# List scatters of the router placed behind three named stages of the scan loop, with a 388-word clearing between them

## The chip, the cores and the metric

The kernel runs on one core of a Trainium2 chip. The metric is the device time of one execution in microseconds (us); lower is better. The core has five engines that run at the same time, each working through its own instructions in order: PE (matrix multiply; its weight loads are shown apart as PEld), DVE (vector operations), ACT (activations and copies), POOL (a general engine, which here also issues all indirect DMAs) and SP (issues the plain DMAs). Sixteen DMA engines carry out the transfers.

## The reference

Two blocks follow each other. The first is a gated linear recurrence over 4 batches of 8 heads, 768 steps, head size 48. The second is a router that sends each of the 3072 resulting rows to two of eight experts.

```python
for t in range(S):                       # attention block
    state = f[:, :, t, :, None] * state + einsum('bhd,bhde' of k_t, v_t)
    y[:, :, t] = einsum('bhd,bhde->bhe', q[:, :, t], state)
x = y.transpose(0, 2, 1, 3).reshape(3072, 384)
noisy = x @ w_gate + log1p(exp(x @ w_noise)) * noise
top2  = the two largest of each row; top2_w = their softmax
for e in range(8):
    out[rows of e] += top2_w * (relu(x[rows] @ w1[e]) @ w2[e])
```

with `f = sigmoid(f_logit)`, w1 of 384 x 1024 and w2 of 1024 x 384 for each expert.

## The kernel before

**The scan loop.** The sequence is cut into 6 chunks of 128 steps; with 4 batches this makes 24 blocks, numbered n = 4 * chunk + batch. The main loop (L1496 to L1566) runs over i and calls, in each turn, seven stages, each for a block of its own (n = i minus the stage's lag): `forget` (transposes of the gate logits on PE, L534, and their logarithm on ACT), `scaled`, `scores`, `summed` (a running sum on DVE, the scan of L548, whose two inputs both lie in SBUF), `output` (PE products of values, L592, and of the carried state, L603, and then the new state on POOL, L619 and L620), `decays`, and `features` (PE product L627, rows to HBM). Behind `forget` stands `clamp` (L528 on POOL), which bounds the gate logits of a later block. The carried state is one per batch: block 23 reads what block 19 wrote, called `st_19` below.

**The lists.** After the four blocks of a chunk, `route(c)`, a generator of which each stage slot runs a step, picks the two experts of every row and their places in the experts' lists. Each chunk then has eight list scatters: `put` (L709) is an indirect DMA on POOL (L711) that writes 128 entries of 16 bytes, and behind each stands a small clearing on POOL: of one word for chunks 0 to 2 (`spacer`, L723), of 388 words in each partition for chunks 3 to 5 (`empty`, L725). The content of both is used by nothing afterwards.

**What sets the order.** Instructions stand on every engine in the order in which the Python code issues them. The loop has a running number `slot` of stage slots, and the condition of L1545 says after which of them a waiting scatter is issued: before the change, every third slot, and every second one once `n_routed` is 3 (= `HALF`) or a first fetch of a list has been issued. When the 24 scatters of chunks 0 to 2 are out, the generator `first_loads` (L1459) issues, some slots later: the fetch of the first list (L872, SP), the eight scatters of chunk 3 in one run, the two gathers of the first list's rows (`xg0`, L885, POOL), and 18 slots on their transposes on PE (`xgp0_0`, `xgp0_1`, L922; the copy behind them, L923, on DVE). Then come the first pieces of the expert part (`hp0_0`, L977).

**The expert part** takes about three quarters of the time; it goes through 256-row pieces of the lists, with the sums of Strassen-like products on DVE and ACT, and scatters the weighted result into `out`.

Of the kernel before, what the change touches and what calls it, by code (L numbers as in the profile page):

```python
# [332 lines left out]
def kernel(  # L333
# [51 lines left out]
    HALF = NCH // 2  # L385
# [133 lines left out]
    def load(nm, n):  # L519
        c, b = n // B, n % B  # L520
        if n < NCH * B:
            nc.sync.dma_start(out=pads[nm][n % RING[nm]][:, :, 0:D],
                              in_={"f": f_logit, "q": q, "k": k, "v": v}[nm][b, :, c * C:(c + 1) * C, :].rearrange("h t d -> t h d"))

    def clamp(n, engine=nc.gpsimd):
        if n < NCH * B:
            raw = pads["f"][n % RING["f"]][:, :, 0:D]
            engine.tensor_scalar(raw, raw, XMIN, None, ALU.max)  # L528
# [107 lines left out]
    def route(c):  # L636
        def t(shape, tag, dtype=F32):
            return rt.tile([128] + shape, dtype, tag=tag, name=f"{tag}_{c}")
# [65 lines left out]
        slot = t([2, B], "slot")  # L704
# [4 lines left out]
        def put(b, r):  # L709
            n_put.append(c)  # L710
            into = nc.gpsimd.indirect_dma_start(  # L711
                out=lists, out_offset=bass.IndirectOffsetOnAxis(ap=sloti[:, r, b:b + 1], axis=0),
                in_=entry[:, c, b, r, :], in_offset=None)
            tc.declare_no_dep(into.ins, group="lists", reason="slots differ")
            tc.add_to_no_dep_group("lists", into.ins)
            if c >= HALF:
                tc.declare_no_dep(into.ins, group="full", reason="slots differ")
                tc.add_to_no_dep_group("later", into.ins)
            if c == NCH - 1:
                tc.declare_no_dep(into.ins, group="nearly full", reason="slots differ")  # L720

            if c < HALF:
                nc.gpsimd.memset(spacer, 0.0)  # L723
            else:
                nc.gpsimd.memset(empty[:, 0:LR // 256], 0)  # L725
# [222 lines left out]
    done = {"fetch": 0, "gather": 0, 1: NR, 2: NR, "turned": False, "joint": False}  # L948
# [502 lines left out]
    def may_put():  # L1451
        return puts and (len(n_put) < HALF * B * 2 or done["fetch"] > (len(n_put) >= (NCH - 2) * B * 2))

    def second_slots():
        fetch(1)
        done["fetch"] = 2
        gather(1, (0,))
# [36 lines left out]
    slot = n_routed = n_first = 0  # L1494
    pieces = chain.from_iterable(((k, i) for i, _ in enumerate(first_layer(k) if k < NE else first_of_three(k))) for k in range(len(items)))
    for i in range(-3, NS + 2):  # L1496
# [5 lines left out]
        for stage, lag in order:  # L1502
            n = i - lag
            if not 0 <= n < NS:
                continue
            stage(n)
            if stage is forget:
                for m in () if n < 2 else (n + 3,) if n < 5 else (n + 3, n + 4) if n == 5 else (n + 4,):
                    load("f", m)
                if n > 1:  # L1510
                    clamp(n + 2)
                if n == 5:
                    tables()
            elif stage is scaled:
                for nm in "qk":
                    load(nm, n + 2) if n < 4 else load(nm, n + 3)
                    if n == 3:
                        load(nm, n + 3)
                if n < 2:
                    load("v", n)  # L1520
            elif stage is scores:
                for m in () if n == 0 else (n + 1,) if n < 4 else (2 * n - 3, 2 * n - 2) if n < 6 else (n + 3,):
                    load("v", m)
                if n in (2, 6, 7, 8, 9, 10):
                    load_router(2 + (2, 6, 7, 8, 9, 10).index(n))
                elif n == 5:
                    nc.sync.dma_start(out=lists.rearrange("(p r) w -> p r w", p=128), in_=empty)
            elif stage is summed and n == 0:
                clamp(2, nc.vector)
            elif stage is output:  # L1530
                while xw:
                    xw.pop(0)()
                if 9 <= n < 17:
                    part_of_weights(0, 1 + (n - 9) // 4, (n - 9) % 4)
                if n == NS - 3:
                    second_slots()
            elif stage is features and NS - 4 <= n < NS - 1:
                if n < NS - 2:
                    for part in range(2):
                        part_of_weights(1, 1, (n - NS + 4) * 2 + part)  # L1540
                zeros(4)
            for _ in range(2 if n_routed >= NCH - 1 else 1):
                next(router, None)
            slot += 1
            if may_put() and slot % (2 if n_routed == HALF or done["fetch"] else 3) == 0:  # L1545
                put_next()
            next(first_pairs, None)

            if done["turned"] and (n_first < 5 or i >= NS - 3 and stage is not forget) and (n_first < 11 or i >= NS - 1):
                next(pieces)  # L1550
                n_first += 1
# [6 lines left out]
        if n >= 0 and n % B == B - 1:  # L1558
            c = n // B
            router = chain(router, route(c))  # L1560
            n_routed = c + 1
# [104 lines left out]
```

## Time and profile before

| | us |
|---|---|
| three timed executions | 616.18, 619.41, 618.79 |
| their median | 618.79 |
| the profiled execution, its own time | 617.76 |
| its span, first to last instruction | 615.7 |
| busy in the span: PE, PEld | 602.0, 553.0 |
| busy in the span: DVE, ACT, POOL | 451.9, 377.8, 290.9 |
| the 48 list scatters on POOL (L711) | 52.8 |
| the 24 one-word and 24 388-word clearings behind them | 2.1 and 10.6 |

The profile is of one execution. Its span is 2.1 us shorter than that execution's time; what lies around the span is taken as fixed. Its rows give the start and the duration of instructions, and behind them in brackets how long the engine was idle before and what ended the idle time ("issue" means that nothing shown in the profile held it). TensorE's granted clock is 0.996 over the span.

### The profile page before, as it was taken

The page shows a single profiled execution, that of the slowest core. Times are in us where ns is not written, and L with a number is a line of the kernel's source. Part 1 is how long each engine was busy: PE and PEld are TensorE (multiplying, and loading weights), DVE is VectorE, ACT ScalarE, POOL GpSimd, SP SyncE. Part 2 cuts the span into 40 slices and gives each one's busy share as a digit, 9 for nine tenths or more (in the row PEclk, how much of TensorE's full clock was granted, in tenths as well). Part 3 has the DMA queues.
Part 4 walks back from the last instruction along what each step waited for, and adds up shares of the span by engine and source line. Part 5 has one row for each costly group of instructions (what it writes and reads, how often), then busy time and mean ns, then how long its engine had stood idle before and what let it go on. Part 6 is the DMA issues. An engine that isn't in the chain of part 4 may idle for free.

```text
span 615.7 us, 13343 instructions
## 1 busy us (share of the span) xinstructions
PE 602.0 (98%) x4830; PEld 553.0 (90%) x4830; DVE 451.9 (73%) x1056; ACT 377.8 (61%) x920; POOL 290.9 (47%) x316
## 2 busy tenths in 40 slices
PE   8999999999999999999999999999999999999995
PEld 7999998887999988998898899889988998998994
DVE  7777878778665488878777778787777777877840
ACT  6877676754222587667666755775577567647611
POOL 7724688878887550451062335414540624242032
PEclk9999999999999999999999999999999999999998
DMA  9999887996973874686489279839874893361024
GB/s 185 187 200 213 174 173 158 206 190 162 327 193 87 142 195 138 142 165 212 138 196 263 65 197 170 259 136 185 159 215 128 199 250 84 82 136 20 2 27 56
DMA packets 186219, 98.79 MB, mean 160 GB/s; under 512 B 150736, under 2 KB 179408, under 8 KB 186144
## 3 DMA queue, kind: packets, MB, share of 16 engines
q1 hardware_dynamic: 173968, 78.59, 51.2%
q0 software_dynamic: 12176, 19.25, 17.2%
q8 instruction: 40, 0.66, 0.4%
q14 instruction: 35, 0.29, 0.2%
HBM read 69.68 MB, written 19.62 MB: 145 GB/s over the span
## 4 chain that ended last, share of the span: by engine, by line
PE 82%; DMA 6%; issue 3%; POOL 3%; ACT 2%; DVE 2%; POOLq 0%; ACTq 0%
PE y L1218 27%; PE E L1052 8%; PE D L1052 8%; PE B L1052 6%; PE C L1052 6%; PE hp L977 5%; PE y L1162 3%; DMA x_rows<-xs 3%; PE sc L574 3%; PE y L592 3%; PE xp L627 2%; PE A L1052 2%; DMA xg<-hs_b 2%; PE fp L534 1%; POOL lists L711 1%
## 5 line engine op out<-in xcount | busy, mean ns | idle before, releaser
L1099 POOL DMA_INDIRECT out_dram<-ys,slots x48 | 91.1, 1898 | 216.0 <-DVE ys L1224 167.6
L1218 PE MATMUL y<-qk_all,f_all 128*128 128x192 f32 x504 | 88.8, 326 | 0.0
L1218 PEld LDWEIGHTS y<-qk_all,f_all 128*128 128x128 f32 x504 | 83.1, 190 | 0.0
L885 POOL DMA_INDIRECT xg<-x_rows,slots x48 | 52.5, 1093 | 36.0 <-DMA slots<-lists 18.8
L1060 ACT ACTIVATE hs_b<-hs_b 128x256 f32<-128x256 f32 x140 | 58.5, 418 | 6.9 <-DVE hs_b L1064 5.2
L1224 DVE SCALAR_TENSOR_TENSOR ys<-y,slots,ys 128x192 f32<-128x192 f32 x63 | 26.1, 415 | 49.1 <-PE y L1218 16.4
L1218 PE MATMUL y<-w,hs_b 128*128 128x192 f32 x336 | 61.5, 326 | 0.0
L711 POOL DMA_INDIRECT lists<-entry,sloti x48 | 52.8, 1101 | 8.7 <-issue 7.4
L1218 PEld LDWEIGHTS y<-w,hs_b 128*128 128x128 f32 x336 | 56.0, 190 | 0.4
L1267 ACT ACTIVATE ys<-y,slots 128x192 f32<-128x192 f32 x21 | 8.9, 421 | 59.5 <-PE y L1218 55.7
L577 DVE TENSOR_TENSOR A<-sc,causal 128x1024 f32<-128x1024 f32 x24 | 29.3, 1221 | 9.0 <-PE sc L574 8.5
L607 ACT COPY yT<-y 128x256 f32<-128x256 f32 x48 | 15.7, 376 | 29.8 <-PE y L603 21.4
L1057 ACT COPY hs_a<-D 128x256 f32<-128x256 f32 x77 | 28.5, 371 | 8.4 <-PE D L1052 4.5
L1218 PE MATMUL y<-qk_all,hs_b 128*128 128x192 f32 x168 | 31.5, 331 | 0.3 <-ACT ys L1239 0.2
L936 ACT COPY planes<-xg 128x768 uint16<-128x768 uint16 x36 | 29.6, 825 | 3.4 <-DMA xg<-x_rows,slots 2.8
L1218 PE MATMUL y<-w,f_all 128*128 128x192 f32 x168 | 31.3, 329 | 0.0
L548 DVE TENSOR_TENSOR_SCAN L<-f,cap 128x512 f32<-128x512 f32 x24 | 29.3, 1221 | 1.4 <-ACT cap L543 1.4
L1057 ACT COPY hs_a<-E 128x256 f32<-128x256 f32 x63 | 23.5, 372 | 10.8 <-PE E L1052 9.5
L1218 PEld LDWEIGHTS y<-qk_all,hs_b 128*128 128x128 f32 x168 | 27.4, 190 | 3.0 <-issue 2.1
L528 POOL TENSOR_SCALAR f_all<-f_all 128x384 f32<-128x384 f32 x21 | 26.4, 1257 | 5.0 <-DMA f_all<-in_f_logit_dram 2.7
L1087 DVE TENSOR_TENSOR f_all<-hs_b 128x512 f32<-128x512 f32 x42 | 28.7, 682 | 0.0
L1218 PEld LDWEIGHTS y<-w,f_all 128*128 128x128 f32 x168 | 27.6, 190 | 0.7
(273 smaller groups left out, 1593.4 us busy)
## 6 DMA issues: line engine op xcount, KB each, us to landing
w<-in_moe_w_dram SPq DMA_DIRECT2D x12, 1536.0 KB
w_q<-in_moe_w_dram SPq DMA_DIRECT2D x10, 1536.0 KB
w<-in_moe_w_dram SPq DMA_DIRECT2D x16, 384.0 KB
f_all<-in_f_logit_dram SPq DMA_DIRECT2D x24, 192.0 KB
qk_all<-in_q_dram SPq DMA_DIRECT2D x24, 192.0 KB
qk_all<-in_k_dram SPq DMA_DIRECT2D x24, 192.0 KB
v_all<-in_v_dram SPq DMA_DIRECT2D x24, 192.0 KB
x_rows<-xs SPq DMA_DIRECT2D x24, 192.0 KB
```

Source lines behind the costliest of these rows:

```text
L548: nc.vector.tensor_tensor_scan(L[n], data0=logf[n], data1=cap[n % 2].rearrange("d a t -> d (a t)"), initial=0.0, op0=ALU.add, op1=ALU.min)
L577: nc.vector.tensor_tensor(A[n].rearrange("j r (a i) -> j (r a) i", i=C), sc.rearrange("j r (a i) -> j (r a) i", i=C), causal.unsqueeze(1). ...
L711: into = nc.gpsimd.indirect_dma_start(out=lists, out_offset=bass.IndirectOffsetOnAxis(ap=sloti[:, r, b:b + 1], axis=0), in_=entry[:, c, b, ...
L885: nc.gpsimd.indirect_dma_start(out=xg[p][:, s, :], out_offset=None, in_=x_rows[0:(known(p) + (p == 1 and s)) * B * C], in_offset=bass.Indi ...
L936: nc.scalar.copy(planes[p][:, s], by_halves(p)[:, s * 2 * DM:(s + 1) * 2 * DM].rearrange("t (d h) -> t h d", h=2))
L977: nc.tensor.matmul(hp[:, o, :], lhsT=w1[home(k)][:, i, (fo + o) * 128:(fo + o + 1) * 128], rhs=rows_of(k)[:, i, :], start=(i == 0), stop=( ...
L1052: nc.tensor.matmul(banks[name, j], lhsT=half_of(x, k)[:, j * 128:(j + 1) * 128], rhs=half_of(y, k), start=first, stop=True, skip_group_che ...
L1057: nc.scalar.copy(at(to, j), banks[more[0], j])
L1060: nc.scalar.activation(at(to, j), at(y, j), AF.Relu, scale=-1.0 if more[0][0] == "-" else 1.0)
L1087: nc.vector.tensor_tensor(sm[which], x, y, op)
L1099: into = nc.gpsimd.indirect_dma_start(out=out, out_offset=bass.IndirectOffsetOnAxis(ap=slots[p][:, s, 2:3], axis=0), in_=ys[s], in_offset= ...
L1218: nc.tensor.matmul(to, lhsT=x[:, o, :], rhs=y[:, o, :], start=(start and o == 0), stop=(o == FH - 1), skip_group_check=not start)
```

## The change

Two lines are changed.

```diff
--- before.py
+++ after.py
@@ -719,7 +719,7 @@
             if c == NCH - 1:
                 tc.declare_no_dep(into.ins, group="nearly full", reason="slots differ")
 
-            if c < HALF:
+            if c == 0:
                 nc.gpsimd.memset(spacer, 0.0)
             else:
                 nc.gpsimd.memset(empty[:, 0:LR // 256], 0)
@@ -1542,7 +1542,7 @@
             for _ in range(2 if n_routed >= NCH - 1 else 1):
                 next(router, None)
             slot += 1
-            if may_put() and slot % (2 if n_routed == HALF or done["fetch"] else 3) == 0:
+            if may_put() and (slot % 2 == 0 if done["fetch"] else stage in (forget, output) or n_routed >= HALF and stage is summed):
                 put_next()
             next(first_pairs, None)
 
```

The first takes the 388-word clearing for chunks 1 and 2 too. The second ties the scatters of chunks 0 to 2 to stages: one behind `forget` and its clamp and one behind `output` in each turn of the loop, and a third behind `summed` once three chunks are routed. The seven stages of a turn gave 2.33 scatters before (3.5 with the shorter step); now they give 2, and later 3. No instruction is added or taken away but for the 16 clearings that are larger; 714 rows stand on POOL before and after.

On POOL, in the turns of chunk 1, the order was this (`sloti_1` holds the places of chunk 1's entries; f_all is a clamp; mid and st are the state of a block):

```order
L528 TENSOR_SCALAR f_all_95<-f_all_95 128x8x48
L711 DMA lists_136<-entry_142,sloti_1_1563 24832x4
L723 MEMSET spacer_147 1x1
L619 TENSOR_TENSOR mid_12_1659<-dss_12_1656,st_8_1195 128x256
L620 TENSOR_TENSOR st_12_1658<-mid_12_1659,P_12_1321 128x256
L711 DMA lists_136<-entry_142,sloti_1_1563 24832x4
L723 MEMSET spacer_147 1x1
L528 TENSOR_SCALAR f_all_95<-f_all_95 128x8x48
L711 DMA lists_136<-entry_142,sloti_1_1563 24832x4
L723 MEMSET spacer_147 1x1
```

Two scatters of chunk 1 stood ahead of the second clamp shown here. In the changed kernel the rows from that same clamp on are these:

```order
L528 TENSOR_SCALAR f_all_95<-f_all_95 128x8x48
L711 DMA lists_136<-entry_142,sloti_1_1561 24832x4
L725 MEMSET empty_137 128x388
L711 DMA lists_136<-entry_142,sloti_1_1561 24832x4
L725 MEMSET empty_137 128x388
L619 TENSOR_TENSOR mid_13_1771<-dss_13_1768,st_9_1311 128x256
L620 TENSOR_TENSOR st_13_1770<-mid_13_1771,P_13_1443 128x256
L711 DMA lists_136<-entry_142,sloti_1_1561 24832x4
L725 MEMSET empty_137 128x388
```

So chunk 1's scatters begin one turn of the loop later (chunk 0's eight now fill the turn before), and all sixteen of chunks 1 and 2 stand between this clamp and the first scatter of chunk 3, where fourteen stood before. From the first scatter of chunk 3 on, POOL's order is the same in both kernels; in both, block 19's state stands behind chunk 3's eight scatters and the two gathers. The end of that run reads, in both:

```order
L711 DMA lists_136<-entry_142,sloti_3_2396 24832x4
L725 MEMSET empty_137 128x388
L885 DMA xg0_2441<-x_rows_135,slots0_2370 128x384
L888 MEMSET empty_137 128x388
L885 DMA xg0_2441<-x_rows_135,slots0_2370 128x384
L888 MEMSET empty_137 128x388
L619 TENSOR_TENSOR mid_19_2481<-dss_19_2478,st_15_2007 128x256
L620 TENSOR_TENSOR st_19_2480<-mid_19_2481,P_19_2127 128x256
L885 DMA xg1_2622<-x_rows_135,slots1_2620 128x384
```

The last scatter of chunk 2 is issued in a later slot than before, and with it `first_loads` and all that it paces. On PE, at the end of the scan loop, the order before was:

```order
L627 MATMUL xp_21_2699<-w_rt_143,yT_21_2616 128x112 x4
L922 MATMUL xgp0_0_2713<-ident_90,xg0_2429 128x128 x3
L592 MATMUL y0_23_2719<-A_23_2660,v_all_97 64x128 x2
...
L603 MATMUL y0_23_2719<-qP_23_2560,st_19_2480 64x128 x2
...
L697 MATMUL rk_4_2740<-each_4_2667,earlier_131 128x32
...
L922 MATMUL xgp0_1_2752<-ident_90,xg0_2429 128x128 x3
L627 MATMUL xp_22_2757<-w_rt_143,yT_22_2695 128x112 x4
L977 MATMUL hp0_0_2770<-xt_a_152,w1_0_148 128x256 x6
```

and it is now:

```order
L627 MATMUL xp_21_2699<-w_rt_143,yT_21_2616 128x112 x4
L592 MATMUL y0_23_2714<-A_23_2660,v_all_97 64x128 x2
...
L603 MATMUL y0_23_2714<-qP_23_2560,st_19_2480 64x128 x2
...
L697 MATMUL rk_4_2735<-each_4_2667,earlier_131 128x32
...
L922 MATMUL xgp0_0_2747<-ident_90,xg0_2441 128x128 x3
L627 MATMUL xp_22_2752<-w_rt_143,yT_22_2695 128x112 x4
L922 MATMUL xgp0_1_2765<-ident_90,xg0_2441 128x128 x3
L627 MATMUL xp_23_2771<-w_rt_143,yT_23_2732 128x112 x4
...
L977 MATMUL hp0_0_2788<-xt_a_152,w1_0_148 128x256 x6
```

The transposes of the gathered rows moved behind block 23's output, which reads `st_19`, and the first expert product `hp0_0` moved behind the last `xp`. The order on SP did not change.

## The prediction

> **What bounds the kernel now.** I read the page's busy times first, then the waits of PE, then the timelines of POOL, DVE and PE around the places where the order changes.
>
> ```profile
> span 615.7 us, 13343 instructions
> PE 602.0 (98%) x4830; PEld 553.0 (90%) x4830; DVE 451.9 (73%) x1056; ACT 377.8 (61%) x920; POOL 290.9 (47%) x316
> PE xgp L922 <- DMA xg<-x_rows,slots: 0.8, 1, 0.8
> PE hp L977 <- DVE xt_a L923: 0.3, 1, 0.3
> ```
>
> PE is busy for 98% of the span, and no PE instruction is added or removed. The time can therefore change only by what PE waits. The two waits shown are the ones in the region that the change reaches: PE waits 0.80 us for the first gathered rows and 0.27 us for their copy. That is 1.07 us in all, and no more can be gained there. What can be lost has no such bound, since PE's work behind this place follows in one chain to the end.
>
> Where these waits lie, on PE, and the POOL run that feeds them:
>
> ```profile
> 147.06 1.15 PE L627 MATMUL xp<-w_rt,yT 128*128 128x112 f32 x8
> 149.01 0.52 PE L922 MATMUL xgp<-ident,xg 128*128 128x128 f32 x3 [0.80 <-DMA xg<-x_rows,slots]
> 149.46 1.09 PE L592 MATMUL y<-A,v_all 128*64 128x128 f32 x16
> 150.48 0.67 PE L603 MATMUL y<-qP,st 64*64 64x128 f32 x16
> 130.03 1.00 POOL L619 TENSOR_TENSOR mid<-dss,st 128x256 f32<-128x256 f32 x1 [1.63 <-ACT dss L612]
> 132.03 1.01 POOL L711 DMA_INDIRECT lists<-entry,sloti  x1 [0.30 <-DVE sloti L707]
> 133.04 0.45 POOL L725 MEMSET empty<- 128x388 uint32 x1
> 133.66 0.98 POOL L711 DMA_INDIRECT lists<-entry,sloti  x1 [0.17 <-issue]
> 145.14 0.99 POOL L885 DMA_INDIRECT xg<-x_rows,slots  x1 [0.16 <-issue]
> 148.89 0.62 POOL L620 TENSOR_TENSOR st<-mid,P 128x256 f32<-128x256 f32 x1
> ```
>
> POOL runs without a pause from 132.03: eight scatters of chunk 3, two gathers, and then block 19's state, `st_19`, done at 148.89 + 0.62 = 149.51. PE's L603 of block 23 reads that state at 150.48, only 0.97 us later. The view shows no wait there, because the wait for the gather stands in front of it.
>
> **The change, part by part.** *The larger clearing and the later start.* For POOL I take the stretch from the clamp at 92.65 (the one with which the second and third order rows begin) to chunk 3's first scatter at 132.03:
>
> ```profile
> 92.65 1.19 POOL L528 TENSOR_SCALAR f_all<-f_all 128x384 f32<-128x384 f32 x1
> 94.02 1.04 POOL L711 DMA_INDIRECT lists<-entry,sloti  x1 [0.18 <-issue]
> L528 POOL TENSOR_SCALAR f_all<-f_all 128x384 f32<-128x384 f32 x5 | 5.9, 1190 | 0.3 <-DMA f_all<-in_f_logit_dram 0.3
> L619 POOL TENSOR_TENSOR mid<-dss,st 128x256 f32<-128x256 f32 x6 | 4.7, 776 | 4.6 <-ACT dss L612 4.6
> L723 POOL MEMSET spacer<- 1x1 f32 x15 | 1.3, 89 | 0.0
> L725 POOL MEMSET empty<- x24: 436/440/462, 133.0 to 181.2; 128x388 uint32 x24
> ```
>
> The middle rows are the groups of POOL in the window 92 to 133; the last is the clearing's line (least, median and longest in ns). Before, this stretch held five clamps, six states and fourteen scatters. In the changed kernel the clamps and states are the same, and there are sixteen scatters. I take the clamp at its old time. It may be earlier or later by part of a microsecond, since what stands ahead of it was reordered too; POOL waits for ACT near there.
>
> - Two more scatters, each with clearing and gap: 133.66 - 132.03 = 1.63, so 3.3 us.
> - Fourteen clearings at 0.44 in place of 0.09: 14 x 0.35 = 4.9 us.
> - Idle time of POOL in the stretch that takes this up: 4.6 us in front of L619 and 0.3 in front of L528. I take all of it, 4.9 us: once POOL is late, ACT's results are ready when it comes.
> - So chunk 3's first scatter is late by 3.3 + 4.9 - 4.9 = 3.3 us, less 0.3 that it waited for `sloti`: **3.0 us**, at about 135.0.
>
> The clearings taken alone would be hidden by the idle time to the last tenth; it is the two scatters pushed into the stretch that come out.
>
> *Scatters that meet a scan.* Their bound is read from DVE's scans beside the slow scatters:
>
> ```profile
> 113.92 1.21 DVE L548 TENSOR_TENSOR_SCAN L<-f,cap 128x512 f32<-128x512 f32 x1
> 114.01 1.98 POOL L711 DMA_INDIRECT lists<-entry,sloti  x1 [0.17 <-issue]
> 121.03 1.22 DVE L548 TENSOR_TENSOR_SCAN L<-f,cap 128x512 f32<-128x512 f32 x1
> 121.34 1.75 POOL L711 DMA_INDIRECT lists<-entry,sloti  x1 [0.18 <-issue]
> 94.03 1.24 DVE L548 TENSOR_TENSOR_SCAN L<-f,cap 128x512 f32<-128x512 f32 x1
> ```
>
> A scatter that starts inside a scan ends about 0.85 us after the scan's end (115.13 to 115.99, 122.25 to 123.09); one that starts just ahead of a scan (94.02) takes 1.04. In the stretch there were two such meetings, worth 0.98 + 0.75 = 1.7 us. The new spacing decides how many there will be. None would make the lateness 3.0 - 1.7 = 1.3 us; two more of 0.8 would make it 4.6. I take the same two, 3.0: a scan fills about 1.2 us of a loop turn of some 6 us, so that one start in five falls into one, and with sixteen scatters two or three meetings are to be expected.
>
> [...]
>
> *What is late next.* Chunk 3's eight scatters, two gathers and `st_19` keep their order, so `st_19` is done at 149.51 + 3.0 = 152.5. On PE, `xgp0_0` now stands behind block 23's output. PE is through with `xp` at 147.06 + 1.15 = 148.2, L592 takes it to 148.2 + (150.48 - 149.46) = 149.2, and then it stands before L603 until 152.5: a **wait of 3.3 us**. The 0.80 in front of `xgp0_0` goes, since the gather is due at 145.14 + 3.0 = 148.1 and landed 149.01 - 145.14 = 3.9 later at most, 152.0. The 0.27 in front of `hp0_0` goes too, because `xp_23`, `more_of` and `total_d` now stand between the copy and that product. Sum on PE: 3.3 - 0.80 - 0.27 = **+2.2 us**. With the bounds 1.3 and 4.6 of the lateness the same sum gives +0.5 and +3.8.
>
> *Other edits at nothing.* A clamp comes later by up to 3 us, but the block that it serves is transposed two turns (some 12 us) on; without that cover PE would wait at L534 for the same 3 us. States 12 to 18 are read four turns after they are written. The router's steps on DVE run beside POOL's backlog.
>
> *The queues behind.* The fetch of the second list on SP waits for chunk 3's scatters to land, and ahead of it SP is idle already; behind it stand weights, zeros and rows:
>
> ```profile
> 147.66 0.38 SPq L872 DMA_DIRECT2D slots<-lists  x1
> 151.35 0.98 POOL L885 DMA_INDIRECT xg<-x_rows,slots  x1 [1.84 <-DMA w<-in_moe_w_dram]
> 157.82 0.48 ACT L632 COPY xs<-xp 128x384 f32<-128x384 f32 x1 [1.11 <-DMA x_rows<-xs]
> 187.64 1.01 POOL L885 DMA_INDIRECT xg<-x_rows,slots  x1 [4.24 <-issue]
> 193.60 0.49 PE L922 MATMUL xgp<-ident,xg 128*128 128x128 f32 x3
> ```
>
> With the 3.0 us, the fetch goes to 150.7 and the last `xs` copy on ACT to 160.8, in front of the relu of `hp0_0`. PE would end that product at about 159.5 and needs its relu only four products of 2.6 us on, so it is covered. POOL works through chunks 4 and 5 without a pause, so the third list's gather moves from 187.64 to 190.6; its rows are transposed at 193.60 + 2.2 = 195.8. At 3.9 us to land (194.5), 1.3 us are left. These are costed at nothing; if the cover is gone, see the second rival.
>
> **Forecast.** Span 615.7 + 2.2 = 617.9, and the profiled execution's 617.76 becomes 620.0. It lies 1.0 below the median of the runs shown, 618.79, which would give 621.0. I predict the middle of the two, 620.5.
>
> **The rivals.** *First: no lateness reaches PE, and the move of `xgp0_0` is a pure gain.* Then the 1.07 us of waits go: 616.7 to 617.7 by the two bases, 617.2. For it: the idle time of POOL nearly pays for the clearings. Against it: two scatters more in the stretch, and `st_19` had only 149.2 - 149.51 = -0.3 us to spare against PE's new order, so that it waits even without lateness. It ends on the side of "not slower" when chunk 3's first scatter is late by less than 0.8 us (0.3 + 0.8 = 1.07). That needs both meetings with a scan to vanish and half a microsecond more. Chance 13%.
>
> *Second: the lateness grows through chunks 4 and 5, and the third list's rows come late for PE.* These scatters run beside DVE's sums with two SBUF inputs, as in the slow rows above; the margin is 1.3 us. Three meetings more at 0.8 us make it -1.1, for both halves at most twice that: 2.2 + 1.1 to 2.2 = some +4, 622.3. Against it: PE's own lateness widens the margin again. Chance 12%.
>
> *Third: scans are held by scatters that started ahead of them.* Three scans in the stretch would find a scatter running if POOL is always busy; at the scatter's 1.0 us each, +3 on the chain from L548 over ACT to the next products, if none of it is covered: 2.2 + 3 = +5.2, 623.5. Against it: the scan of 94.03 at 1.24 us. Chance 4%. [...]
>
> **How the numbers follow.** Forecast 71%, with a range of its own of 618.5 to 622.5 (+0.5 to +3.8 and about 0.2 for the base). The range for 8 in 10 runs down to 617.2, where the first rival stands, and up to 623.2, past the second: **617.2 to 623.2**. A measurement of this kernel can tell a change of about 0.5%, 3.1 us, from none; the three runs shown span 3.2. The forecast of +2.2 lies within that, and crosses it only with one or two meetings more, about 2 in 10 of its 71%, which is 14%; with most of the second and third rival, slower by over 0.5% has 26%. The first rival's 1.07 us is under 0.2%, so that faster by over 0.5% needs an unusual pair of runs as well: 6%. Within 0.5%: 68%.
>
> **What would show it.** In the profile after, PE's waits should name L603 of block 23 waiting for POOL's `st` (L620), some 3 us, and no longer L922 for `xg`, nor L977 for `xt_a`. Chunk 3's first scatter should stand near 135 in place of 132.03 and wait for nothing on DVE; POOL's idle time in front of L619 between 92 and 133 should fall from 4.6 us to near zero; the clearings should take 0.44 each. Scatters of 1.2 us and more should each begin inside a scan. If PE waits little at L603 but the time rises, the second or third rival holds (L922 for the third list's `xg`, or scans over 1.3 us). The prediction is wrong if POOL reaches chunk 3 before 132.8.

## The result, and the profile after

| | us |
|---|---|
| before, median of 6 executions (least to most) | 618.5 (616.18 to 620.06) |
| after, median of 6 executions (least to most) | 627.08 (626.17 to 629.91) |
| ratio, with its 95% interval | 1.0144 (1.0109 to 1.0180) |
| predicted | 620.5 (617.2 to 623.2) |

The change makes the kernel slower by 1.4%, some 8.6 us. The prediction had the sign right in its sum (+2.2) and the place right, but a quarter of the size; the time lies outside its range, and "within 0.5%" was the wrong class.

The page of the changed kernel begins so (span and busy times):

```profile
span 625.4 us, 13344 instructions
PE 605.8 (97%) x4830; PEld 556.0 (89%) x4830; DVE 454.2 (73%) x1056; ACT 377.5 (60%) x920; POOL 295.1 (47%) x316
```

PE is busy for 605.8 us where it was busy for 602.0, with the same 4830 products. So a part of the loss is no wait at all: some products took longer. The first two rows of PE's waits (total, times, longest):

```profile
PE y L603 <- POOL st L620: 5.6, 1, 5.6
PE E L1052 <- ACT xt_b L1298: 1.9, 1, 1.9
```

The first is the wait that was forecast, at the forecast place, with 5.6 us in place of 3.3. The second was not foreseen. PE's timeline through the first (start, duration, line, in brackets the idle time before):

```profile
146.98 1.09 PE L592 MATMUL y<-A,v_all 128*64 128x128 f32 x16
153.68 1.13 PE L603 MATMUL y<-qP,st 64*64 64x128 f32 x16 [5.61 <-POOL st L620]
...
156.28 1.89 PE L627 MATMUL xp<-w_rt,yT 128*128 128x112 f32 x8
...
161.69 10.61 PE L977 MATMUL hp<-xt_a,w 128*128 128x256 f32 x48
...
172.49 1.55 PE L1162 MATMUL y<-w,hs_a 128*128 128x192 f32 x8
```

The eight records of L627 (products for `xp`) take 1.89 us behind the wait, against 1.15 at 147.06 before the change. The windows of two microseconds tell why (length, busy time of PE, PEld, DVE, ACT and POOL, then the granted clock of TensorE, DMA share and GB/s):

```profile
148.00:150.00 2.00, 0.07 (x2) 0.00 (x0) 0.26 (x2) 0.70 (x2) 1.84 (x3) 1.00 0.02 1
150.00:152.00 2.00, 0.00 (x0) 0.00 (x0) 0.00 (x0) 0.00 (x0) 1.84 (x4) 0.69 0.41 69
152.00:154.00 2.00, 0.32 (x8) 0.32 (x12) 0.00 (x0) 0.00 (x0) 1.54 (x3) 0.50 0.90 249
...
160.00:162.00 2.00, 2.00 (x15) 1.98 (x15) 1.39 (x3) 0.48 (x1) 1.72 (x3) 0.75 1.07 371
```

The granted clock falls to 0.50 while PE stands idle, and is back at 1.00 only at about 161. Before the change it was 1.00 in all these windows, of which this is one:

```profile
152.00:154.00 2.00, 1.73 (x13) 1.48 (x12) 1.93 (x7) 0.48 (x1) 1.69 (x3) 1.00 1.06 378
```

POOL in the same kernel, in the stretch from the clamp at 92.57 to block 19's state; the first row is the group of L619 in the window 92 to 137:

```profile
L619 POOL TENSOR_TENSOR mid<-dss,st 128x256 f32<-128x256 f32 x6 | 4.4, 737 | 0.0
99.97 2.01 POOL L528 TENSOR_SCALAR f_all<-f_all 128x384 f32<-128x384 f32 x1
106.00 1.43 POOL L620 TENSOR_TENSOR st<-mid,P 128x256 f32<-128x256 f32 x1
120.79 1.85 POOL L711 DMA_INDIRECT lists<-entry,sloti  x1 [0.16 <-issue]
128.26 1.43 POOL L620 TENSOR_TENSOR st<-mid,P 128x256 f32<-128x256 f32 x1
133.04 1.66 POOL L711 DMA_INDIRECT lists<-entry,sloti  x1 [0.17 <-PE y L603]
...
136.68 1.02 POOL L711 DMA_INDIRECT lists<-entry,sloti  x1 [0.16 <-issue]
149.26 0.99 POOL L885 DMA_INDIRECT xg<-x_rows,slots  x1 [0.16 <-issue]
153.00 0.62 POOL L620 TENSOR_TENSOR st<-mid,P 128x256 f32<-128x256 f32 x1
```

Chunk 3's first scatter stands at 136.68, late by 4.65 us against 132.03; the prediction had 3.0. The five rows behind the group's are the operations that took longer than their kind. POOL stood idle for 0.0 us in front of L619, where it had been 4.6.

How far PE is behind, at four places that both kernels have:

| PE at | before | after | behind by |
|---|---|---|---|
| L603 of block 23 | 150.48 | 153.68 | 3.20 |
| first y of item 0 (L1162) | 165.69 | 172.49 | 6.80 |
| first E product (L1052) | 216.98 | 225.63 | 8.65 |
| B of the same (L1052) | 220.37 | 229.67 | 9.30 |
| end of the span | 615.7 | 625.4 | 9.7 |

So there are three pieces: 3.2 us of lateness, 3.6 us right behind it, and 2.5 us at a second place. At this second place PE waits for the transposed halves of later rows. SP's queue, first in the changed kernel, then before:

```profile
208.74 2.58 SPq L939 DMA_TRANSPOSE xg<-hs_b  x1
211.38 1.34 SPq L872 DMA_DIRECT2D slots<-lists  x1
212.89 2.61 SPq L939 DMA_TRANSPOSE xg<-hs_b  x1
```

```profile
202.14 1.52 SPq L939 DMA_TRANSPOSE xg<-hs_b  x1
203.72 0.93 SPq L872 DMA_DIRECT2D slots<-lists  x1
205.02 2.86 SPq L939 DMA_TRANSPOSE xg<-hs_b  x1
```

The first of them is later by 6.60 us, as PE is by then. But issuing it took 1.06 us longer and the fetch behind it 0.41, so that the second is later by 7.87. ACT could use it at 223.63 (214.85 before), which is later by 8.78: another 0.9 us went by between issue and use. PE waited 1.89 us, and behind this wait, too, a window shows the clock at half:

```profile
225.63 1.03 PE L1052 MATMUL E<-xt_b,w 128*128 128x256 f32 x2 [1.89 <-ACT xt_b L1298]
```

```profile
226.00:228.00 2.00, 2.00 (x6) 1.35 (x4) 1.90 (x7) 2.00 (x5) 1.67 (x1) 0.50 0.00 0
```

### The profile page after: what moved, and what is told of

Its sections match the earlier page's. It is cut to its first block, busy times and chain, and to the rows that moved or that the text cites. A ratio compares the mean times of both kernels' runs of the same rounds, so it can differ in the third digit from the quotient of the medians.

```text
span 625.4 us, 13344 instructions
## 1 busy us (share of the span) xinstructions
PE 605.8 (97%) x4830; PEld 556.0 (89%) x4830; DVE 454.2 (73%) x1056; ACT 377.5 (60%) x920; POOL 295.1 (47%) x316
## 4 chain that ended last, share of the span: by engine, by line
PE 83%; POOL 10%; issue 2%; DMA 2%; SPq 1%; ACT 1%; DVE 0%; POOLq 0%; ACTq 0%
PE y L1218 29%; PE E L1052 8%; PE D L1052 8%; PE C L1052 6%; PE B L1052 6%; PE hp L977 5%; POOL lists L711 4%; PE y L1162 3%; PE xp L627 2%; PE sc L574 2%; PE y L592 2%; PE A L1052 2%; DMA xg<-hs_b 2%; POOL f_all L528 2%; POOL empty L725 2%
## 5 line engine op out<-in xcount | busy, mean ns | idle before, releaser
L885 POOL DMA_INDIRECT xg<-x_rows,slots x48 | 51.0, 1063 | 35.8 <-DMA slots<-lists 20.1
L711 POOL DMA_INDIRECT lists<-entry,sloti x48 | 51.4, 1070 | 10.9 <-issue 7.2
L607 ACT COPY yT<-y 128x256 f32<-128x256 f32 x48 | 15.6, 376 | 33.3 <-PE y L603 26.0
L627 PE MATMUL xp<-w_rt,yT 128*128 128x112 f32 x192 | 29.0, 297 | 0.1
```

Source lines behind the costliest of these rows:

```text
L627: nc.tensor.matmul(xp[:, hp, :], lhsT=yT[n][:, hp % 2, cols(hp // 2)], rhs=w_rt[:, hp, :], start=True, stop=True)
L711: into = nc.gpsimd.indirect_dma_start(out=lists, out_offset=bass.IndirectOffsetOnAxis(ap=sloti[:, r, b:b + 1], axis=0), in_=entry[:, c, b, ...
L885: nc.gpsimd.indirect_dma_start(out=xg[p][:, s, :], out_offset=None, in_=x_rows[0:(known(p) + (p == 1 and s)) * B * C], in_offset=bass.Indi ...
```

## The experiments

The theory from here on: POOL is late at what PE needs next (block 19's state, the first gathered rows); PE's idle time then costs a second time through its clock. The rivals: the new order costs by itself, or the clearings do, or the lower clock has another cause or no price. Each run is given as a ratio to the kernel before, measured on the same chip at the same time.

| run | ratio | 95% interval |
|---|---|---|
| order alone | 1.0008 | 0.9976 to 1.0040 |
| clearing alone | 0.9985 | 0.9965 to 1.0006 |
| change, 40 idle products in the wait | 1.0121 | 1.0085 to 1.0157 |
| change, state first | 1.0193 | 1.0119 to 1.0266 |
| change, 22 idle products | 1.0093 | 1.0065 to 1.0121 |
| change, chunk 2 with one-word clearing | 1.0001 | 0.9975 to 1.0027 |
| change, state and gathers first | 1.0112 | 1.0073 to 1.0151 |
| change, one-word clearing for chunks 1 to 3 | 1.0106 | 1.0076 to 1.0137 |
| before, three more clearings | 1.0061 | 1.0038 to 1.0084 |
| before, six more clearings | 1.0092 | 1.0063 to 1.0121 |
| before, one-word clearing for chunk 3 too | 1.0164 | 1.0136 to 1.0191 |
| order alone, state first | 1.0033 | 1.0007 to 1.0059 |

### Each half of the change alone

The first run has the second hunk of the diff only (the stages), the second run the first hunk only (`if c == 0`).

> The new order of the scatters, with the one-word clearing for chunks 1 and 2 as before. Theory (POOL's lateness at block 19's state is the cause, and the order by itself costs PE nothing): 16 clearings at 0.35 us less make 5.6 us, of which about 1 comes back as idle time in front of L619; chunk 3's first scatter stands near 132, block 19's state is done near 149, PE waits 0 to 1.5 us at L603 of block 23, the granted clock stays at 1.00 from 150 to 162, and PE waits less than 0.5 us at L1052 near 225. Time 616 to 618.5. Rival (the order itself is the cause, by its crowding of scatters and loads): chunk 3's first scatter near 136 or PE's waits and lower clock as in the changed kernel; time 622 or more.

> The 388-word clearing for chunks 1 and 2, in the old order. Theory: 14 clearings at 0.35 us (4.9) go into the 4.9 us in which POOL stood idle there; what comes out is up to two meetings with scans. Chunk 3's first scatter at 132.0 to 133.7, the first gather as late as it, and PE waits for the gathered rows at L922 0.8 to 2.5 us (0.80 before); the clock stays at 1.00. Time 618.5 to 620.5. Rival (the clearings alone make the lateness): chunk 3's first scatter at 135 or later, PE waits over 4 us at L922, the clock falls; time 624 or more.

POOL at chunk 3's first scatter, with the order alone and then with the clearing alone; and PE's waits of each:

```profile
130.35 1.01 POOL L711 DMA_INDIRECT lists<-entry,sloti  x1 [0.15 <-issue]
```

```profile
131.04 1.02 POOL L711 DMA_INDIRECT lists<-entry,sloti  x1 [0.16 <-issue]
```

```profile
PE y L603 <- POOL st L620: 1.7, 1, 1.7
```

```profile
PE xgp L922 <- DMA xg<-x_rows,slots: 3.3, 2, 1.7
```

Neither half makes POOL late: the scatter comes at 130.35 and 131.04, earlier than the 132.03 before the change, while both together bring it to 136.68. (For the clearing alone 132.0 to 133.7 had been expected.) Neither half costs time that can be measured. In both the clock stayed at 1.00. PE waited 1.74 us with the order alone, a little more than the 0 to 1.5 expected, because it had arrived earlier (146.4). So the two halves don't add up: the two shifts make 2.7 us earlier, both edits together make 4.65 later. Of these 7.3 us, 4.9 is POOL's idle time, which pays for the one or for the other, not for both. Most of the rest is scans: the operations held by one took 2.0 us longer than their kind in this stretch before the change, 3.2 with the order alone, 0.4 with the clearing alone and 3.95 with both.

### The clock by itself

The changed kernel, with products on PE that nobody reads, ahead of L603 of block 23 (40 in the first run, 22 in the second):

```diff
+        if n == NCH * B - 1:
+            keep = one_bank("keep")
+            for _ in range(40):
+                nc.tensor.matmul(keep[:, 0:128], lhsT=ones, rhs=ones, start=True, stop=True)
```

> The changed kernel with 40 products of 128 x 128 whose result nobody reads, on PE just ahead of L603 of block 23 (about 4.4 us of work at full clock, in the time in which PE stood idle). Nothing else is added. Theory (after several idle us PE is granted half its clock, and this is a cost of its own): block 23's L603 still starts near 153.7, but its own wait is about 1 us, the granted clock from 152 to 162 is 0.95 or more, item 0's first y comes about 3 us earlier than in the changed kernel, and the time is 622.5 to 625 (627.1 less 3, less up to 1.5 at the second place near 225). Rival (the lower clock has another cause, or costs nothing since weight loads bound the products): the clock falls as before or the products are as fast as before; time 626.5 to 627.5.

> As the run with 40 idle products, but with 22. The 40 took 9.2 us (0.23 each), 3.4 us more than the wait that they were to fill; 22 should take 5.1 us and end before block 19's state is ready, so that L603 of block 23 starts near 153.7, just as in the changed kernel. The two kernels then differ by PE's clock alone. Theory (the half clock after the wait is a cost of its own): the clock is 0.95 or more from 152 to 162, the first expert product starts near 158.3 (161.69 in the changed kernel), and the time is 620 to 622.5 (the run with 40 measured 624.5; less 3.4 is 621.1). Rival (the filler only changed other things by its overshoot): the first expert product starts near 161 or later, time 624 or more.

With the 40 products, PE's timeline (L607 here is the L603 of the other kernels), and one window:

```profile
147.99 9.20 PE L603 MATMUL keep<-ones 128*128 128x128 f32 x80
157.12 0.67 PE L607 MATMUL y<-qP,st 64*64 64x128 f32 x16
161.79 10.61 PE L981 MATMUL hp<-xt_a,w 128*128 128x256 f32 x48
```

```profile
152.00:154.00 2.00, 2.00 (x20) 2.00 (x19) 0.00 (x0) 0.00 (x0) 1.78 (x4) 1.00 0.58 158
```

I had taken 4.4 us for them, which no run shows; they took 9.2 (80 records, two for each product), so that L603 came 3.44 us later than in the changed kernel, at 157.12. Even so the first expert products start at 161.79, as in the changed kernel (161.69). From L603 to there it is 4.67 us with the clock at 1.00 and 8.01 with the clock at half: **3.34 us is the price of the half clock**, read from the same work in two kernels. With PE kept busy by these products and nothing else changed the clock stayed at 1.00 (0.50 from 152 to 154 without them), so that here it was the idle time that lowered it.

The 22 products were to take the overshoot away. They took 5.18 us, but PE reached them only at 151.73, and L603 stood at 156.84:

```profile
146.67 0.45 PE L592 MATMUL y<-A,v_all 128*64 128x128 f32 x4 [0.30 <-issue]
148.25 0.49 PE L607 MATMUL y<-qP,st 64*64 64x128 f32 x8 [0.34 <-issue]
156.84 0.67 PE L607 MATMUL y<-qP,st 64*64 64x128 f32 x16
161.51 2.84 PE L981 MATMUL hp<-xt_a,w 128*128 128x256 f32 x12
```

The rows have short stalls that nothing in the profile accounts for; I come back to them. From L603 to the first expert products it is 4.67 us again, but the time that I expected (620 to 622.5) was missed: 625.15, with 619.74 for the kernel before on that chip. In the two runs the clock's price is shown by the rows; as a gain in the whole time it isn't, since both intervals overlap that of the change.

### The named wait taken away

The changed kernel with other pauses in `first_loads`:

```diff
-        for what, p, pause in (("fetch", 1, 4), ("first", 0, 0), ("second", 0, 18), ("turned", 0, 0)):
+        for what, p, pause in (("fetch", 1, 6), ("first", 0, 0), ("second", 0, 16), ("turned", 0, 0)):
```

Block 19's state then stands on POOL behind chunk 3's second scatter; PE's order is the same.

> The changed kernel with the run of chunk 3's scatters and the first list's gathers two stage slots later, so that block 19's state stands on POOL behind the second of those scatters and not behind the gathers. PE's order is the same. Theory (POOL as a whole is late, and the state is only the first of two things that PE needs from it): the wait at L603 of block 23 is 0; the gather goes from 149.3 to about 150.8, its rows land near 154.5, and PE waits 4 to 5 us at L922 instead; the clock falls as before; time 625.5 to 627.5. Rival (only the place of the state behind the gathers is the cause): with it PE waits less than 1.5 us in all there, the clock stays at 1.00; time 616 to 619.

PE's waits, the first row:

```profile
PE xgp L922 <- DMA xg<-x_rows,slots: 8.0, 2, 5.7
```

This is the change's chief wait, 5.6 us, taken away whole, and the time is no better (627.57, ratio 1.0193). PE goes through L603 at 147.80 and stands 5.69 us before the gathered rows, and then 2.32 before the second half. POOL as a whole was late; the wait in the list named only what was asked of it first.

### Half of the larger clearing

The changed kernel, with the one-word clearing for chunk 2 again:

```diff
-            if c == 0:
+            if c in (0, HALF - 1):
                 nc.gpsimd.memset(spacer, 0.0)
```

> The changed kernel with the one-word clearing behind chunk 2's scatters, the 388-word one still behind chunk 1's: 8 x 0.35 = 2.8 us less on POOL. Theory (POOL's spare time takes up one of the two edits, and PE's wait grows with what is over; the clock falls only after a longer wait): chunk 3's first scatter at 132.5 to 134.5 (136.68 with both edits whole, 130.35 with the order alone), PE waits 2 to 4 us at L603 of block 23, the clock is 0.95 or more from 150 to 162, and the time is 617 to 619.5 on the scale on which the kernel before has 616.2 to 618.5. Rival (any wait above some 2 us costs the clock too): the clock falls to 0.5 for several us, time 620 to 623.

The first scatter of chunk 3 on POOL, and PE at L603 of block 23:

```profile
133.72 1.75 POOL L711 DMA_INDIRECT lists<-entry,sloti  x1 [0.15 <-issue]
```

```profile
151.44 0.67 PE L603 MATMUL y<-qP,st 64*64 64x128 f32 x16 [0.44 <-POOL st L620]
```

Chunk 3's first scatter came where it was expected (133.72 within 132.5 to 134.5), and the time is that of the kernel before. But the wait at L603 was 0.44 us, not 2 to 4: PE itself was 1.95 us later than with the order alone two blocks ahead (141.83 against 139.88 at L603 of block 21), and then had stalls like those above. PE also waited 1.26 us for the second half of the gathered rows (L922), and the clock stayed at 1.00. So the run shows that 2.8 us less on POOL are enough to undo the loss; it doesn't show the size of a middle wait.

### Lateness alone

The kernel before, with three and with six clearings more, in `first_loads` ahead of the loop that issues chunk 3's scatters:

```diff
+                for _ in range(3):
+                    nc.gpsimd.memset(empty, 0)
```

> The kernel before, with three more clearings on POOL (776 words in each partition, an estimated 0.76 us each from the 0.44 of 388 words and the 0.60 of 580) ahead of chunk 3's scatters, and nothing else: POOL is late by 2.3 us there. Theory (lateness of POOL at this place is enough by itself): chunk 3's first scatter near 134.4, PE waits about 3.1 us for the first gathered rows at L922 (0.80 before). If the clock stays up at a wait of this length, ratio 1.002 to 1.005; if it falls, as it did behind a wait of 3.1 us in another run, 1.006 to 1.010. Rival (the changed kernel lost its time by something else than lateness of POOL): no more than 1 us of wait, ratio 1.000 to 1.002.

> As the run with three more clearings, but six: POOL is late by 4.6 us, as in the changed kernel. Theory: chunk 3's first scatter near 136.7, PE waits about 5.4 us at L922, the granted clock falls to 0.5 for 6 us or more, which costs some 3 us more, and the ratio is 1.010 to 1.017, as in the changed kernel (1.0144), with order and clearings of the kernel before. Rival (lateness alone is not enough): ratio under 1.008, or the clock stays at 1.00.

PE's wait and a window behind it, with three clearings and then with six:

```profile
151.97 0.52 PE L922 MATMUL xgp<-ident,xg 128*128 128x128 f32 x3 [2.77 <-DMA xg<-x_rows,slots]
```

```profile
154.00:156.00 2.00, 2.00 (x22) 1.67 (x18) 0.13 (x1) 0.65 (x2) 0.77 (x2) 0.50 1.01 361
```

```profile
152.56 0.87 PE L922 MATMUL xgp<-ident,xg 128*128 128x128 f32 x3 [2.57 <-DMA xg<-x_rows,slots]
```

```profile
152.00:154.00 2.00, 1.44 (x9) 1.14 (x11) 0.64 (x2) 0.48 (x1) 1.66 (x3) 0.50 1.04 278
```

One thing was not as expected: chunk 3's first scatter had been issued ahead of the clearings, at 132.40 and 131.39, and not near 134.4 and 136.7. The second scatter shows the lateness, 136.43 and 137.83 in place of 133.66. Three clearings gave a wait of 2.77 us and 0.61% (expected 3.1 us; 0.6 to 1.0% if the clock falls, which it did). With six, the first gather came 3.71 us later than before, but PE was later itself and waited 2.57 us only, not 5.4, and the ratio of 1.0092 lies just under the expected 1.010. In both PE was behind by far more than by the wait: L922 starts 2.96 and 3.55 us later than before (149.01), the first y of item 0 5.69 and 7.03 us later. Lateness of POOL alone, with the old order and the old clearings, makes 0.61 and 0.92% of the change's 1.44%, and in the profiles about half of it comes behind the wait.

The mean clock is not lower in every execution. Of the ten with three clearings, three had a mean granted clock of 0.996 or 0.997 and took 619.5 to 620.3 us; the six with 0.993 or less took 622.0 to 624.7. That is a difference of some 3.9 us within one kernel on one chip, and it is the clock's price as it stands in the whole time, as far as nothing else differs between these executions.

### Versions that should have won

Three runs put what PE needs earlier. The first is the run with the state first, with the two gathers ahead of chunk 3's last four scatters:

```diff
-                while puts and len(n_put) < (NCH - 2) * B * 2:
+                while puts and len(n_put) < HALF * B * 2 + 4:
                     put_next()
                 gather(p, (0,))
             elif what == "second":
                 gather(p, (1,))
                 done["gather"] = p + 1
+                while puts and len(n_put) < (NCH - 2) * B * 2:
+                    put_next()
```

The second is the changed kernel with one-word clearings for chunks 1 to 3 (`if c <= HALF:`); the third is the order alone with the pauses of 6 and 16 slots.

> The changed kernel with both of the things that PE needs from POOL ahead of most of chunk 3's scatters: block 19's state behind the second of them, the two gathers of the first list behind the fourth, the other four after them. PE's order is that of the changed kernel. Theory (PE's loss is nothing but the lateness of these two): state done near 141, first rows landed near 148.3, PE waits 0 to 0.5 us between 146 and 160, the clock stays at 1.00, and the time is 2 to 3 us under the kernel before (1.07 us of its waits gone and the earlier scan loop kept, 1.4): ratio 0.995 to 0.998. Rival (what is put back is missed later: the second list's fetch now stands behind four scatters that come 3.2 us later): PE waits over 1.5 us for rows of the second or third list, ratio 1.000 or more.

> The changed kernel's order with the one-word clearing for chunks 1 and 2 and for chunk 3 too (8 x 0.35 = 2.8 us less behind chunk 3's first scatter). Theory: chunk 3 begins near 130.4 as with the order alone, the first gather stands near 141, block 19's state is done near 145.3, ahead of PE (146.4), so that the wait of 1.74 us that the order alone had is gone and the clock stays at 1.00; time 1 to 3 us under the kernel before, ratio 0.995 to 0.999. Rival (the larger clearing behind chunk 3's scatters spaces them for the sake of the transfers, and without it scatters or loads take longer): scatters above 1.2 us without a scan, rows landing over 4.5 us after the gather, ratio 1.000 or more.

> The run of the order alone (one-word clearing for chunks 1 and 2, 388 words for chunk 3), with chunk 3's run two slots later, so that block 19's state stands behind its second scatter. Theory: the 1.74 us that PE waited at L603 of block 23 with the order alone go, the rows are gathered near 145.2 and landed near 149.1, so that PE waits 0 to 0.7 us at L922; ratio 0.994 to 0.999. Rival (PE is then held by something else within the next 10 us, as in the runs that put work ahead): ratio 1.000 or more.

None of the three won: the ratios are 1.0112, 1.0106 and 1.0033, in the range of the rivals, but only the first and the last for reasons like those that the rivals gave. With the state and the gathers first the rows landed in time, but the second list's fetch now stood on SP behind chunk 3's last scatters (156.11, 150.49 after the change), and the stores of rows behind the fetch. The rows of waits show what hung on them, ACT first, then PE:

```profile
ACT xs L632 <- DMA x_rows<-xs: 12.1, 1, 12.1
```

```profile
PE rk L697 <- DVE each L680: 3.1, 1, 3.1
PE more_of L740 <- DVE f_all L734: 1.0, 1, 1.0
```

ACT could not write the next rows (`xs`) for 12.1 us, the last router steps behind it on ACT and DVE were late, and PE waited 3.1 us for `each` at 172.07; the clock was at half twice. This is the queue that the prediction had costed at nothing, with its cover gone. With state first on the order alone, PE waited 1.47 us at 152.62 for the second half of the rows, and the clock fell in the profiled execution. In four others of that run the mean clock was 0.996 or 0.997, and they took 617.2 to 619.5 us, as the kernel before does there (median 618.44). With the small clearings PE had no wait there for any engine; its products simply came slowly, from 133 to 144.5, which neither theory had named:

```profile
138.80 0.47 PE L534 MATMUL kp<-ident,qk_all 128*128 128x128 f32 x1 [0.61 <-issue]
142.36 1.08 PE L574 MATMUL sc<-qP,kQ 64*128 64x128 f32 x3 [1.03 <-issue]
```

That run differs from the order alone (1.0008) in the clearing behind chunk 3's scatters and in nothing else. To see whether this belongs to the new order, the kernel before got the same edit:

```diff
-            if c < HALF:
+            if c <= HALF:
                 nc.gpsimd.memset(spacer, 0.0)
```

> The kernel before with the one-word clearing behind chunk 3's scatters too, nothing else. Theory A (the larger clearing there keeps the scatters apart, and without it PE's instructions come late, as in the run with the new order and one-word clearings for chunks 1 to 3): PE stands idle 2 us or more between 130 and 150 with nothing in the profile that held it, ratio 1.005 or more. Theory B (what was seen in that run belongs to its order of the work, not to the spacing of chunk 3): the gather comes 2.8 us earlier, the wait of 0.80 at L922 goes, ratio 0.996 to 1.001.

PE's timeline and one window of this kernel:

```profile
143.12 0.37 PE L574 MATMUL sc<-qP,kQ 64*128 64x128 f32 x1 [0.68 <-issue]
144.54 0.49 PE L592 MATMUL y<-A,v_all 128*64 128x128 f32 x2 [0.35 <-issue]
```

```profile
142.00:146.00 4.00, 2.18 (x10) 1.05 (x8) 0.00 (x0) 1.78 (x5) 3.51 (x5) 0.50 0.44 53
```

The slow products don't belong to the new order: the ratio here is 1.0164, about as much as the whole change costs (1.0144), by an edit that takes work away. In four microseconds PE has 10 records of products where the kernel before has 64 in the same window. So the 388-word clearing behind chunk 3's scatters is worth its 2.8 us: with it scatters stand 1.57 us apart, without it 1.27. How a denser run of scatters would slow PE's products is open; the profile names no releaser, and the DMA share is 0.44 there. That their distance does it is a reading: no run changes it apart from the clearing.

## Why the prediction was wrong, point by point

**In short.** The forecast was +2.2 us, and PE is 9.3 us behind at B of L1052. Three steps failed: the lateness of POOL was too small (about 1 us of the difference on PE); "The time can therefore change only by what PE waits" left out that products can slow down (3.6 us right behind the wait, PE's busy time up by 3.8); and "the queues behind", at nothing, cost 2.5 us.

**What bounds the kernel, and where: right as to the place.** The two waits of 0.80 and 0.27 us went, as the sum had it. The wait came at L603 of block 23, on `st` of L620.

**The clearings and the idle time: right.** They take 0.44 us each; POOL's idle time in front of L619 in the stretch went from 4.6 us to 0.0. "The clearings taken alone would be hidden by the idle time" is what the run with the clearing alone shows.

**The lateness of 3.0 us: too small, 4.65.** The step of that sum that failed is "scatters that meet a scan": I counted two meetings, 1.7 us, as before (a third, 0.26 us on L619 at 130.03, I had overlooked). There were five. Two were scatters (0.85 and 0.66 more than 1.0). The other three were operations for which I had allowed none: a clamp (2.01 in place of 1.19) and two states (1.43 in place of 0.62). Together they are 3.95, or 2.3 more than I took. Of this some 0.6 came back, mainly because two other terms were too large: from start to start a larger clearing took 0.32 us more than a small one, not 0.35, and a scatter with its clearing 1.50, not 1.63. My own reason should have led there: a POOL that never rests meets a scan with whatever it is doing, not with scatters only. The trace bears that out: the clamp of 99.97 and the states of 106.00 and 128.26 each started inside a scan (99.81 to 101.02, 105.53 to 107.01, 127.51 to 129.27).

**PE's arrival at L603, 149.2: too late, 148.07.** I took PE's place in the loop from the trace of before. With the new order its loop ran ahead (the `sc` products that end the loop start at 142.99 in place of 144.35), in part because a wait of 0.61 us for `yT` at 97.27 was gone. A wait grows at both ends: state later by 1.1 than forecast (153.62 in place of 152.5; of the 4.65 on POOL 0.5 had gone again, since no scatter of chunk 3 was held by a scan, as one at 139.97 had been), PE earlier by 1.1, wait 5.6 in place of 3.3. In the sum only the first counts; at L603 PE is 3.20 us behind and not the forecast 2.0.

**The clock: missing.** No term and no rival of the prediction had it. It is 3.3 of the 3.6 us between L603 and item 0's first y; the other 0.3 is there with the clock at 1.00 too (the run with 40 products) and goes with the new order of PE's work. I had seen 0.97 us of wait at 219 without any loss of clock, and took products behind a wait at their durations ahead of it. The trace has the clock at 0.50 in and behind a wait of 5.61; it fell at 150.77, when PE had been idle for 2.70 us. The forecast wait of 3.3 us, with its range to 4.9, was over three times the 0.97 behind which I had seen the clock hold, so that a lower clock behind it should have been a rival. In the runs it stayed at 1.00 behind 1.74 us (order alone) and was at 0.50 behind 2.77 (three more clearings).

**"The queues behind" at nothing: wrong at one place.** The third list's rows kept their margin (the changed kernel's list of waits has none at L922). Behind them the second transfer of halves came late, which I had not looked at: 1.89 us of wait and the clock at half for another 3.4 us, 2.5 us in all. The rows show SP taking 1.06 us longer to issue the first transfer of halves and 0.41 longer for the fetch behind it. Why, is open: in the run with 40 products the same three rows take 1.53, 0.97 and 2.73 us with PE as far behind, and PE didn't wait.

**The rivals.** The first (a pure gain) fell with the lateness. The second had the right turn, a second late transfer, at another place. The third is not what happened to PE, and no run shows the 1.0 us for each scan that its sum uses: the scan that started with the scatter of 93.94 took 1.25 us in the changed kernel, against the usual 1.21. Scans that started inside an L619 took 1.48 (at 105.53) and 1.76 us (at 127.51, 0.08 behind it), and none of PE's listed waits names one.

**The chances.** "Slower by over 0.5%" had 26%. With the clock's step in the list, a wait of over 3 us would have carried its own 3 us (3.34 by the run with 40 products), and most of the forecast's range would have moved into that class.

## What to carry to other kernels

Idle time of an engine is a purse that can be spent once: two edits that are each free against it can cost everything together (here chunk 3's first scatter at 130.35 and 131.04 with one edit, at 136.68 with both), so cost them as one sum, with every operation of the busier engine, not only the moved ones. A wait that is named in the profile is the first thing asked of a late engine; take it away, and if the engine is still late the next thing is waited for (here 5.61 us at L603, then 5.69 at L922). And price a new wait of PE with the clock behind it: here the slow products behind waits of 2.6 to 5.6 us cost 2.7 to 3.5 us more.

## What was not expected of the hardware

**The half clock came in steps of 3.41 us.** From windows of half a microsecond in each run, the times at which the granted clock fell and rose:

| run | fell | rose | length | wait of PE there |
|---|---|---|---|---|
| the change, first | 150.77 | 161.01 | 10.24 | 5.61 |
| the change, second | 225.86 | 229.28 | 3.42 | 1.89 |
| state first | 151.76 | 168.82 | 17.06 | 5.69 and 2.32 |
| state and gathers first | 154.15 | 160.98 | 6.83 | 0.36 and 0.95 |
| the same, second | 171.22 | 178.05 | 6.83 | 3.09 |
| three more clearings | 153.11 | 159.94 | 6.83 | 2.77 |
| six more clearings | 150.89 | 161.13 | 10.24 | 2.57, short stalls |
| order alone, state first | 154.36 | 161.19 | 6.83 | 1.47 |
| one-word for chunks 1 to 3 | 137.50 | 151.15 | 13.65 | short stalls |
| before, one-word for chunk 3 | 138.78 | 152.43 | 13.65 | short stalls |

Every length is a multiple of 3.41 us to within 0.02, and in one run the changes of the clock lie on one grid (161.01 to 225.86 is 19 times 3.413). Idle time as long as such a step was not needed for it: 1.47 us of idle time was followed by 6.83 us at half clock, and in the changed kernel the clock fell 2.70 us into the idle time. Nor does the length of a wait decide alone, since 1.74 us (order alone) and 1.70 and 1.55 us close together (clearing alone) left the clock at 1.00. What else decides is open.

**Eight scatters in a run 1.27 us apart go with slow products on PE.** It was seen in both pairs of kernels that differ in the clearing between these scatters alone (1.0008 and 1.0106; 1.0000 and 1.0164). The pairs of scatters some 1.3 us apart in chunks 1 and 2 of the kernel before (94.02 and 95.36 is one) left PE without such stalls: its waits from 90 to 133 are 0.6 and 0.2 us, both for ACT. Shorter stalls stand in some of the other runs: 0.30 and 0.34 us with the 22 products, 1.58 us apart (146.67, 148.25) where the scatters stand 1.57 apart, and 0.24 and 0.32 with one-word clearing for chunk 2 and with six more clearings, 3.90 and 0.73 us apart.

**Clamps and states were held by a scan as scatters are**, in the changed kernel by 0.8 us each: a clamp took 2.01 us (1.19 at 92.57) and two states 1.43 (0.62 at 153.00), each begun inside a scan.
